# A fused convolution and feed-forward kernel: head slots shifted, chunks of 103 tokens

## The chip, the cores and the metric

One core of one Trainium2 chip. The metric is the device time of one execution in microseconds (us). The kernel before takes 484.77 us (median of 3 runs, 483.08 to 486.48). These three spread by 0.7%.

## The reference, cut to what matters

```python
# x: (8, 4160, 192), 8 heads of 24 channels, 7 taps per head, softmax over the taps
x_pad = concat(zeros(B, 6, D), x)                       # causal
conv[b, s, h, :] = sum_k w[h, k] * x_pad[b, s + k, h, :]
# then a feed-forward layer on the 33,280 tokens, 192 -> 768 -> 192
h = max(max(y @ w1, y @ w2), y @ w3)
out = h @ w_out
```

## The kernel before

Tokens are worked through in 65 blocks of 512. For each block the convolution runs on TensorE: a chunk of x (tokens in partitions) is the stationary operand, a banded matrix of the taps is the moving one, and the result comes out with channels in partitions. A chunk of n output tokens needs n + 6 input rows, and the rows of a chunk are the partitions of its load.

```python
CHK = P - PAD                       # 128 - 6 = 122 tokens, so 128 rows
...
for o_lo in range(0, N, CHK):       # 4 x 122 + 24
    o_hi = min(o_lo + CHK, N)
    row_lo = max(0, S + o_lo - PAD)
    rlen = min(P, SEQ - row_lo)
...
# load_x(t): all chunks of a block with one transfer where the rows allow it
src = bass.AP(tensor=x.tensor, offset=row[i] * D,
              ap=[[D, rlen], [step * D, k - i + 1], [1, D]])
nc.sync.dma_start(out=xf[0:rlen, i:k + 1, :], in_=src)
```

Each head's 24 channels fill a slot of 32 partitions, four slots to a PSUM bank. After evacuation to half precision (`ys`), transfers move the slots to a dense layout (`yd`, 64 channels in three columns), and one more transfer copies the lower 64 partitions to the upper 64, so that the matmuls of the two halves overlap: in the trace of before the 1170 `lp` and the 1170 `lq`, of 64 rows each, are busy 316.5 and 315.1 us, and together 347.5 us.

```python
def repack(t):                      # 10 pieces of 24, 16 or 8 rows
    for n, (half, s0, c, r0, rows) in enumerate(pieces):
        (nc.sync, nc.gpsimd)[n % 2].dma_start(out=yd[r0:r0 + rows, c, :],
                                              in_=slots[t][s0:s0 + rows, half, :])
def double(t):
    nc.sync.dma_start(out=dense[t][HALF:P, :, :], in_=dense[t][0:HALF, :, :])
...
for t in range(1, NB):
    u = t + AHEAD                   # AHEAD = 3
    load_x(t + 7)                   # sync queue
    cast_x(t + 5)                   # GpSimd
    double(u - 1)                   # sync queue
    l1(t, 0)                        # first matmuls of block t
    ...                             # conv(u), every second t for two blocks; evacuation
    repack(u)                       # sync queue and GpSimd
    ...                             # the rest of block t and of the second layer of t - 1
    store(t - 1, 0, 4, (nc.gpsimd,))
```

The softmax here doesn't subtract the row's maximum and nothing guards it: scores larger than these inputs give would overflow.

## Time and profile before

| | before |
|---|---|
| time | 484.77 us |
| TensorE busy | 470.7 us of 482.2 |
| period of two blocks | 14.0 us |
| x load of a block | 480 KB, 640 rows of 768 B |
| moves of a block's repack | 10 (5 sync queue, 5 GpSimd) |

One view is added here: the sync queue's instructions in order of time (start, duration, engine, line, kind, what goes where, how many).

```profile
65.66 0.54 SPq L365 DMA_DIRECT2D yd<-yd  x1
66.30 3.59 SPq L359 DMA_DIRECT2D yd<-ys  x5
69.93 0.52 SPq L123 DMA_DIRECT2D xf<-in_x_dram  x1
```

A block is one copy to the upper half, five moves of the repack and one load. The durations are those of issuing, not of moving data: 640 rows are issued in 0.52 us, and the last raise of such a load's semaphore comes 4.3 us after its issue (median).

### The profile page before, as it was taken

The page shows a single profiled execution, that of the slowest core. Times are in us where ns is not written, and L with a number is a line of the kernel's source. Part 1 is how long each engine was busy: PE and PEld are TensorE (multiplying, and loading weights), DVE is VectorE, ACT ScalarE, POOL GpSimd, SP SyncE. Part 2 cuts the span into 40 slices and gives each one's busy share as a digit, 9 for nine tenths or more (in the row PEclk, how much of TensorE's full clock was granted, in tenths as well). Part 3 has the DMA queues.
Part 4 walks back from the last instruction along what each step waited for, and adds up shares of the span by engine and source line. Part 5 has one row for each costly group of instructions (what it writes and reads, how often), then busy time and mean ns, then how long its engine had stood idle before and what let it go on. Part 6 is the DMA issues. An engine that isn't in the chain of part 4 may idle for free.

```text
span 482.2 us, 22628 instructions
## 1 busy us (share of the span) xinstructions
PE 470.7 (98%) x9083; PEld 394.6 (82%) x9083; DVE 367.3 (76%) x609; ACT 327.7 (68%) x608; POOL 279.1 (58%) x465
## 2 busy tenths in 40 slices
PE   7899999989999999999999999999999999999995
PEld 3478888878888888888888888888888888888995
DVE  6667877767778778777877777777877787787774
ACT  5676667756667676667677676766667666766663
POOL 2676656755655665575566557376755655676301
PEclk9899999999999999999999999999999999999999
DMA  8857756756666676666666676577665665664323
GB/s 203 242 153 201 197 155 190 204 152 186 199 185 184 175 200 183 177 191 176 194 198 190 190 193 190 159 196 215 201 170 167 207 189 164 194 164 112 95 83 100
DMA packets 77260, 85.86 MB, mean 178 GB/s; under 512 B 13472, under 2 KB 65160, under 8 KB 77156
## 3 DMA queue, kind: packets, MB, share of 16 engines
q1 hardware_dynamic: 59554, 52.74, 40.5%
q0 software_dynamic: 17248, 31.39, 21.0%
q8 instruction: 71, 1.16, 1.0%
q10 hardware_dynamic: 354, 0.30, 0.2%
q14 instruction: 33, 0.27, 0.2%
HBM read 34.04 MB, written 25.56 MB: 124 GB/s over the span
## 4 chain that ended last, share of the span: by engine, by line
PE 93%; DMA 3%; ACT 1%; DVE 1%; SPq 1%; issue 0%; POOL 0%; POOLq 0%
PE lp L376 30%; PE po L419 29%; PE lq L376 25%; PE G L310 7%; DMA yd<-yd 2%; DMA yd<-ys 1%; PE D L330 1%; PE idle L189 1%; SPq L359 1%; ACT r L380 0%; PE band_sum L234 0%; ACT band L257 0%; POOL yd L359 0%; ACT w3h L251 0%; DVE h L381 0%
## 5 line engine op out<-in xcount | busy, mean ns | idle before, releaser
L381 DVE TENSOR_TENSOR h<-r,lq 128x512 f16<-128x512 f16 x390 | 267.0, 685 | 103.5 <-ACT r L380 103.4
L380 ACT ACTIVATE r<-lp 128x512 f16<-128x512 f32 x390 | 232.7, 597 | 135.9 <-PE lp L376 93.8
L376 PE MATMUL lq<-yd,wd 64*128 64x512 f16 x1170 | 315.1, 375 | 1.8 <-DMA yd<-yd 1.3
L376 PE MATMUL lp<-yd,wd 64*128 64x512 f16 x1170 | 316.5, 377 | 0.1
L419 PE MATMUL po<-wo,h 64*128 64x192 f16 x3120 | 231.5, 243 | 0.0
L419 PEld LDWEIGHTS <-h 64*128 64x128 f16 x3120 | 187.2, 94 | 25.7 <-issue 0.2
L376 PEld LDWEIGHTS <-wd 64*128 64x128 f16 x2340 | 163.0, 93 | 26.0 <-DMA yd<-yd 2.9
L359 POOL DMA_DIRECT2D yd<-ys x315 | 161.6, 520 | 6.0 <-DMA yd<-ys 2.9
L445 POOL DMA_DIRECT2D out_dram<-o x64 | 51.3, 802 | 175.5 <-DVE o L429 145.0
L419 PE MATMUL po<-m,yd 64*128 64x192 f16 x780 | 87.0, 243 | 0.0
L429 DVE TENSOR_TENSOR o<-a,po 128x384 f32<-128x384 f32 (+1 forms) x132 | 71.3, 541 | 0.6 <-ACT a L428 0.6
L139 POOL CAST x<-xf 128x960 f16<-128x960 f32 (+3 forms) x71 | 64.2, 911 | 4.1 <-DMA xf<-in_x_dram 2.7
L428 ACT COPY a<-po 128x384 f32<-128x384 f32 (+1 forms) x132 | 61.8, 469 | 1.2 <-PE po L419 1.2
L419 PEld LDWEIGHTS <-yd 64*128 64x128 f16 x780 | 55.0, 94 | 6.1
L310 PEld LDWEIGHTS <-x 128*32 128x32 f16 (+1 forms) x2544 | 33.2, 97 | 13.0 <-issue 12.8
L341 ACT CAST ys<-G 128x512 f16<-128x512 f32 x66 | 36.3, 588 | 4.6 <-PE G L310 1.2
L341 DVE CAST ys<-G 128x512 f16<-128x512 f32 x60 | 38.5, 683 | 0.6 <-DMA yd<-ys 0.2
L310 PE MATMUL G<-band,x 128*32 128x122 f16 (+1 forms) x2544 | 36.4, 210 | 0.0
L154 POOL CAST xz<-xf 128x240 f16<-128x240 f32 (+2 forms) x6 | 2.4, 448 | 11.7 <-DMA xf<-in_x_dram 11.7
L189 PE MATMUL idle<-idle 128*128 128x512 f16 x14 | 6.1, 580 | 1.2 <-DVE unit L201 1.2
L189 PEld LDWEIGHTS <-idle 128*128 128x128 f16 x14 | 1.6, 131 | 3.6 <-issue 2.1
L330 PEld LDWEIGHTS <-xz 128*32 128x32 f16 x240 | 3.5, 102 | 1.3 <-issue 1.3
(43 smaller groups left out, 39.5 us busy)
## 6 DMA issues: line engine op xcount, KB each, us to landing
out_dram<-o POOLq DMA_DIRECT2D x64, 384.0 KB
xf<-in_x_dram SPq DMA_DIRECT2D x48, 480.0 KB
yd<-yd SPq DMA_DIRECT2D x63, 192.0 KB
yd<-ys SPq DMA_DIRECT2D x189, 24.0 KB
yd<-ys POOLq DMA_DIRECT2D x189, 24.0 KB
xf<-in_x_dram SPq DMA_DIRECT2D x8, 384.0 KB
xf<-in_x_dram SPq DMA_DIRECT2D x8, 288.0 KB
xf<-in_x_dram SPq DMA_DIRECT2D x8, 192.0 KB
```

Of the source, the lines that this page charges most:

```text
L139: nc.gpsimd.tensor_copy(out=x16[0:rl, q0:q1, :], in_=xf[0:rl, q0:q1, :])
L189: nc.tensor.matmul(ps[:], lhsT=idle[:, 0:P], rhs=idle[:], start=True, stop=True)
L310: nc.tensor.matmul(G[h // 4][32 * g:32 * g + 32, lo:hi], lhsT=x16[0:rlen, q, cb:cb + 32], rhs=band[0:rlen, h, cc:cc + hi - lo], start=True ...
L341: copy(out=slots[t][:, i, :], in_=convs[t][i][:])
L359: (nc.sync, nc.gpsimd)[n % 2].dma_start(out=yd[r0:r0 + rows, c, :], in_=slots[t][s0:s0 + rows, half, :])
L376: nc.tensor.matmul(ps[i][:, 0:N], lhsT=wd[row, c, P * j:P * (j + 1)], rhs=y[row, c, 0:N], start=(c == 0), stop=(c == NC - 1))
L380: nc.scalar.activation(out=r[:, 0:N], in_=ps[0][:, 0:N], func=AF.Relu)
L381: nc.vector.tensor_max(out=hs[t][:, j, 0:N], in0=r[:, 0:N], in1=ps[1][:, 0:N])
L419: nc.tensor.matmul(ps[b0, i][:, s % 2, :], lhsT=a, rhs=b, start=first, stop=last)
L428: nc.scalar.copy(out=a[:, ss, :], in_=ps[s0, 0][:, ss, :])
L429: nc.vector.tensor_add(out=outs[t][:, s0:s + 1, :], in0=a[:, ss, :], in1=ps[s0, 1][:, ss, :])
L445: qs[i].dma_start(out=bass.AP(tensor=out.tensor, offset=r * D, ap=[[D, n], [step * D, s1 - s0], [1, D]]), in_=ob[p0:p0 + n, s0:s1, :])
```

## The change

The intent is to have fewer and larger moves. Even heads are put at the end of their slot and odd heads at its start, so two neighbours touch and move together as 48 rows; the 10 moves become 6. To allow it the x tiles get 8 spare columns at each end. With it the chunks become even: 103, 103, 103, 103 and 100 tokens instead of 4 x 122 + 24.

```diff
-CHK = P - PAD
+CHK = 103
...
-                rlen = min(P, SEQ - row_lo)
+                rlen = min(CHK + PAD, SEQ - row_lo)
...
-            for h in range(NHEAD):
-                g = h % 4
-                cb = GRP * h if h < NHEAD - 1 else GRP * h - 8
-                nc.tensor.matmul(
-                    G[h // 4][32 * g:32 * g + 32, lo:hi],
-                    lhsT=x16[0:rlen, q, cb:cb + 32],
...
+            for i in range(2):
+                for g in range(4):
+                    h = SLOTS[i][g]          # ((0, 1, 2, 3), (6, 7, 4, 5))
+                    cb = q * D + GRP * h + EDGE * (g % 2)
+                    nc.tensor.matmul(
+                        G[i][32 * g:32 * g + 32, lo:hi],
+                        lhsT=x16[0:rlen, cb:cb + 32],
...
+    pieces = ((0, 8, 0, 0, 48), (0, 72, 0, 48, 16), (0, 88, 1, 0, 32),
+              (1, 72, 1, 32, 32), (1, 104, 2, 0, 16), (1, 8, 2, 16, 48))
```

Cut: the four x tiles in half precision become constants with their edges set to zero, and the cast writes between the edges.

More of the change, by code (lines that the diff above doesn't have):

```diff
@@ L87 @@
     xfp = ctx.enter_context(tc.tile_pool(name="xfp", bufs=6))
-    x16p = ctx.enter_context(tc.tile_pool(name="x16p", bufs=4))
     ysp = ctx.enter_context(tc.tile_pool(name="ysp", bufs=4))
@@ L100 @@
     NDENSE, AHEAD = 2, 3
+    SLOTS = ((0, 1, 2, 3), (6, 7, 4, 5))
+    EDGE = 32 - GRP
     xin = {}
+    nlast = len(chunks_of[NB - 1])
+    x16s = [const.tile([P, NQ * D + 2 * EDGE], FP16, name=f"x16_{i}") for i in range(4)]
+    x16z = const.tile([P, nlast * D + 2 * EDGE], FP16, name="x16_z")
     def load_x(t):
@@ L135, in cast_x @@
         n = len(chunks_of[t])
-        x16 = (x16p.tile([P, NQ, D], FP16, tag="x16", name=f"x16_{t}") if n <= NQ else
-               const.tile([P, n, D], FP16, name=f"x16_{t}"))
+        x16 = x16s[t % 4] if n <= NQ else x16z
+        v = x16[:, EDGE:EDGE + n * D].rearrange("p (q d) -> p q d", d=D)
         for (rl, q0, q1) in parts:
-            nc.gpsimd.tensor_copy(out=x16[0:rl, q0:q1, :], in_=xf[0:rl, q0:q1, :])
+            nc.gpsimd.tensor_copy(out=v[0:rl, q0:q1, :], in_=xf[0:rl, q0:q1, :])
         xin[t][1] = x16
@@ L195 @@
     nc.gpsimd.memset(xz[1][:], 0.0)
+    for x16 in x16s + [x16z]:
+        w = x16.shape[1] - EDGE
+        nc.gpsimd.memset(x16[:, 0:EDGE], 0.0)
+        nc.gpsimd.memset(x16[:, w:w + EDGE], 0.0)
     unit = const.tile([P, 32 + 2 * PAD], FP16)
@@ L306, in conv @@
         for (q, b, row_lo, rlen, lo, hi, cc) in chunks_of[t]:
-            for h in range(NHEAD):
-                g = h % 4
-                cb = GRP * h if h < NHEAD - 1 else GRP * h - 8
-                nc.tensor.matmul(
-                    G[h // 4][32 * g:32 * g + 32, lo:hi],
-                    lhsT=x16[0:rlen, q, cb:cb + 32],
-                    rhs=band[0:rlen, h, cc:cc + hi - lo],
-                    start=True, stop=True, tile_position=(0, 32 * g))
+            for i in range(2):
[5 more added lines that the diff above has]
+                        lhsT=x16[0:rlen, cb:cb + 32],
+                        rhs=band[0:rlen, h, cc:cc + hi - lo],
+                        start=True, stop=True, tile_position=(0, 32 * g))
         slots[t] = ysp.tile([P, 2, NBLK], FP16, tag="ys", name=f"ys_{t}")
@@ L341, in evac @@
         copy(out=slots[t][:, i, :], in_=convs[t][i][:])
-    pieces = []
-    for h in range(NHEAD):
-        s0 = 32 * (h % 4) + (8 if h == NHEAD - 1 else 0)
-        ch = GRP * h
-        while ch < GRP * (h + 1):
-            n = min(GRP * (h + 1), HALF * (ch // HALF + 1)) - ch
-            pieces.append((h // 4, s0 + ch - GRP * h, ch // HALF, ch % HALF, n))
-            ch += n
+    pieces = ((0, 8, 0, 0, 48), (0, 72, 0, 48, 16), (0, 88, 1, 0, 32),
+              (1, 72, 1, 32, 32), (1, 104, 2, 0, 16), (1, 8, 2, 16, 48))
     def repack(t):
```

## The prediction

> **What bounds the kernel now.** I read the head of the page first, then the chain that ended last, then the groups kept apart by shape.
>
> ```profile
> PE 470.7 (98%) x9083; PEld 394.6 (82%) x9083; DVE 367.3 (76%) x609; ACT 327.7 (68%) x608; POOL 279.1 (58%) x465
> ...
> q1 hardware_dynamic: 59554, 52.74, 40.5%
> q0 software_dynamic: 17248, 31.39, 21.0%
> ...
> PE 93%; DMA 3%; ACT 1%; DVE 1%; SPq 1%; issue 0%; POOL 0%; POOLq 0%
> ```
>
> TensorE is the bound: busy in 98% of the span and 93% of the chain. The windows view of 60 to 74 us and 200 to 214 us shows PE busy 14.00 of 14.00 us at clock 1.00. Two blocks of 512 tokens take 14.0 us there, so a block takes **7.0 us**, and 65 blocks with start and end make 482 us. The transfers are hidden: 40.5% + 21.0% of the 16 engines' time. That is an average over 16 engines, and the argument below turns on its not staying one.
>
> What the change touches, by shape:
>
> ```profile
> L359 POOL DMA_DIRECT2D yd<-ys x315 | 161.6, 520 | 6.0 <-DMA yd<-ys 2.9 <-issue 1.8 <-ACT ys L341 0.7
> L310 PE MATMUL G<-band,x 128*32 128x122 f16 x1984 | 34.6, 219 | 0.0
> L310 PE MATMUL G<-band,x 128*32 128x24 f16 x432 | 11.6, 175 | 0.0
> L139 POOL CAST x<-xf 94x192 f16<-94x192 f32 x8 | 2.8, 352 | 1.4 <-DMA xf<-in_x_dram 1.4
> ```
>
> The repack is 10 moves per block, 5 issued from GpSimd at 520 ns and 5 from the sync queue at 740 ns (median of the line's view). Neither queue is full. The last row is the only load with an odd row count, and it is the clue.
>
> **How a load is spread over the engines.** [...]Counting its semaphore records between a transfer's issue and its landing, a 128-row load raises its semaphore 16 times; the 94-row load (94 = 2 x 47) 3 times, one of them 0.5 us after issue[...] and two at 4.3 to 5.9 us; the 70-row load 15 times (14 engines + 1); the 24-row moves of the sync queue 13 times (12 + 1); the 8-row ones 9 (8 + 1). Some 10% of the small moves show fewer raises than their kind's number; one 70-row load and the eight 94-row loads are the only odd ones[...].
>
> The DMA view of 254.9 to 255.3 us, in the tail of a 94-row load, shows how fast two engines are:
>
> ```profile
> DMA packets 28, 0.02 MB, mean 56 GB/s; under 512 B 2, under 2 KB 27, under 8 KB 28
> ...
> q1 hardware_dynamic: 28, 0.02, 19.5%
> ```
>
> 27 - 2 = 25 packets are of 768 B (192 floats: one row of one chunk). On two engines over 0.4 us that is 0.4 x 2 / 25 = 32 ns each. In another such tail the packet records are two trains, each with a packet every **33 ns**. One engine moves one 768 B row per 33 ns.
>
> **The trap in the change.** A chunk of 103 tokens with its 6 rows before it is 109 rows, and **109 is prime**. The instruction order of the changed kernel shows every x load of the first 64 blocks on the sync queue as 109x5x192 (or 109x2 and 109x3). [...]all 5 x 109 = 545 packets of a block go through engine 0. Before, 5 x 128 = 640 packets went over 16 engines, 40 each, about 1.4 us.
>
> **The change part by part, per block.**
> - x load: 545 x 33 ns = **18.0 us** on engine 0. That alone is more than twice PE's 7.0 us, so it can't be hidden. It saves 15% of the bytes, which is worthless here.
> - Other traffic of engine 0: from the packet records (median alone): repack 192 rows x 1 KB = 12 packets per engine x 46 ns = 0.55; the copy to the lower half 4 packets of 3 KB x 121 ns = 0.48; store 5 packets of 4.6 KB x 178 ns and a smaller one of 65 ns = 0.95; about ten increments of 9 ns = 0.1. Sum 2.1 us. The new repack pieces of 16, 32 and 48 rows all use 16 engines, so this part is well spread.
> - So engine 0 needs **20.1 us per block** against PE's 7.0.
> - Repack: 4 fewer issues: 2 x 740 ns on the sync queue, 2 x 520 ns on GpSimd. None lies on the path before (GpSimd is 58% busy) and none will after.
> - Conv: still 40 pairs of weight load and matmul per block, 512 columns in all; 4 x 122 + 24 becomes 4 x 103 + 100. The chain gives 1.06 us for a pair of blocks (80 matmuls), 13 ns each. Even chunks can move this by some 0.1 us a block, at most 6 us, and it is hidden under 20 us.
> - Casts: 960 elements per partition as before, 0.99 us; ten tiny memsets at the start.
>
> **Does engine 0 stay fed?** At the start of the kernel before, loads are issued faster than they drain:
>
> ```profile
> 5.18 0.60 SPq L123 DMA_DIRECT2D xf<-in_x_dram  x1
> 7.27 0.37 SPq L179 DMA_DIRECT2D wos<-in_moe_w_out_dram  x1
> 7.69 8.50 SPq L123 DMA_DIRECT2D xf<-in_x_dram  x4
> ```
>
> Four issues take 8.50 us instead of 4 x 0.52. [...]rows issued less packets started, at the end of each held issue, come to 123 to 126 per engine. So a load of 545 rows holds the sync queue until some 124 are left, 124 x 33 ns = 4.1 us of work. In that time it must issue the copy (0.53), three repack moves (3 x 0.74) and the next load, whose first packet comes 1.18 us after its issue starts (spacing seen on isolated loads): 0.53 + 2.2 + 1.18 = 3.9 us. It just fits, and the copy and repack packets add 0.75 us of cover. Gaps of up to 1 us a block are possible. The repack's evacuations are ready long before, since PE works only 7 of 20 us.
>
> **The sum.** First packet at 1.9 us; x packets of 64 blocks 64 x 18.0 = 1151; weights' share of engine 0 some 6 (some 110 rows of 768 B to 2 KB); other traffic of the 57 blocks finished meanwhile 57 x 2.1 = 120. The copy of block t+2 is issued behind the load of block t+7 in the same ring, so PE enters block 58 only when the load of block 63 is through: 1279 us. From there PE runs as before: block 58 starts at about 427 us of 482, so 55 us remain, plus 2 for the copy's landing. 1279 + 57 = 1336. I add 14 for gaps and for a PE that may be cold after each wait: **1350 us**, 2.8 times the time before.
>
> **Rivals.**
> - *The spread is not what I think* (the next dimension is used, or a ragged split over 16 engines). Then 409 KB per block are hidden as 480 were, and only fewer DMAs, even conv chunks and smoother starts count. DMA waits on PE's own records are 1.7 us in all, so 476 to 484 us: within 2%. For it: 94 and 70 rows show divisors, but no prime count is in this trace. Against: 94 gave 2 and not 16, though 16 engines were there, and 24 gave 12. I give it 6%.
> - *Engine 0 starves between loads*: the sync queue waits for a repack to land before the copy, and then first packets come late: 1.2 to 2 us per block, 64 x 1.5 = 96, about 1430 us.
> - *Rows are slower than 33 ns in a long train.* With all 16 engines on loads at 13.3 to 16.2 us, 1242 packets take 2.9 x 16 / 1242 = 37 ns each, which would make 64 x 545 x 37 = 1290 and 1475 in all. [...]alone two engines kept 33, so I hold it unlikely.
> - *DVE, ACT or GpSimd as new bound*: no; they do the same work as before in a longer time, and would be some 25% busy.
>
> **Range and chances.** Both slower rivals set the top of the range, 1460; the bottom, 1300, is the sum with 32 ns and less other traffic. Faster 0.01, same 0.05, slower 0.94.
>
> **What would show it.** PE busy near 35% (471 of 1350 us; more where a colder clock stretches it), its idle put down to DMA (yd<-yd above all), and a clock below 1 in slices. The sync queue's line of x loads with a median near 14 us in place of 0.5. Of all engines' time the DMA share down to some 16% (18 + 16 x 2.1 = 52 of 16 x 20.1 us a block), and mean bandwidth near 60 GB/s (85.9 MB less 15% of the loads' 31 MB, over 1350 us). A period of 20 us per block instead of 7. Two raises of the semaphore per x load, the first at once, the second some 20 us later. Wrong if x loads still land in 4 us, or if the period is far from 20 us: at 18 the other traffic overlaps, at 22 or more the ring ran dry.

The sum: 1.9 + 1151 + 6 + 120 = 1279, plus 57 is 1336, plus 14 is 1350 us. What the trace of before shows is the count of raises: 16 for 128 rows, 3 for 94, 15 for 70, and in the sync queue's moves 13 for 24 rows and 9 for 8. 94, 70, 24 and 8 rows raise once more than their largest divisor up to 16. For the 94-row loads one raise comes 0.5 us after the issue, and the first packet of an isolated load only after 1.18 us, so I count the others as engines, and 16 raises as 16. That 109 rows would leave one engine was my estimate from these counts; no prime row count was in that trace, and the changed kernel's trace shows it below. "Engine 0" is a name for that one engine, as no trace names a packet's engine, and "ring" one for the queue. That 16, 32 and 48 rows use 16 engines is read from 16 raises each in the sync queue of the changed kernel. That a colder TensorE stretches its work shows there too: the same 9083 matmuls keep it busy 609.4 us at a mean granted clock of 0.709, against 470.7 us at 0.995 before.

## More of the kernel before

Where the data's arrival matters, it shows in somebody's wait. Of who waited for whom, two of the lines, GpSimd's casts for x and TensorE's first matmuls for the copy, are:

```profile
POOL x L139 <- DMA xf<-in_x_dram: 2.7, 4, 1.4
...
PE lq L376 <- DMA yd<-yd: 1.3, 2, 1.1
```

These are totals over the whole execution in us, number of times, and the longest. Both are small, so the transfers are hidden.

## The result, and the profile after

The changed kernel takes **1338.04 us** (median of 4 runs, 1337.43 to 1338.99), against 485.26 us for 4 runs of before. The ratio is 2.7589 (95% interval 2.7484 to 2.7693). A ratio here is the mean time of one kernel's fast runs over that of the other's of the same rounds, so it is not quite the ratio of the medians.

From the head of the page of the changed kernel: busy time by engine, the two main queues (packets, MB, share of 16 engines) and the chain by engine.

```profile
PE 609.4 (46%) x9083; PEld 432.7 (32%) x9083; DVE 374.8 (28%) x609; ACT 333.6 (25%) x608; POOL 212.6 (16%) x341
...
q1 hardware_dynamic: 51894, 48.27, 12.7%
q0 software_dynamic: 13216, 31.38, 6.3%
...
DMA 63%; SPq 27%; PE 4%; issue 3%; POOL 1%; POOLq 0%; ACT 0%; DVE 0%
```

TensorE does the same 9083 matmuls and is busy 46% instead of 98%. The transfers' share of all engines has fallen from 61.5% to 19.0%, and yet the chain is 63% transfers. Low mean use of 16 engines and a bound by transfers do not exclude each other: one engine can be full. The DMA view of 605 to 611 us, inside one x load, shows it:

```profile
DMA packets 181, 0.14 MB, mean 23 GB/s; under 512 B 4, under 2 KB 179, under 8 KB 181
...
q1 hardware_dynamic: 174, 0.13, 6.5%
```

For 6 us on end the core moves 23 GB/s, and the share is 6.5%, which is one sixteenth (6.25%). 174 packets in 6 us are one per 34 ns. Of who waited for whom, the lines that answer to those of before:

```profile
POOL x L146 <- DMA xf<-in_x_dram: 551.8, 62, 17.0
...
PE lq L383 <- DMA yd<-yd: 629.3, 57, 28.4
```

GpSimd's cast waits for x 62 times, and TensorE waits 57 times, once a block, for the copy. The copy is not slow in itself (with the loads in another queue, in e10 below, it lands 5.1 us after its issue; here 19.3, medians). It stands behind a load of x in the same queue, which the sync queue's order of time shows:

```profile
618.58 13.50 SPq L372 DMA_DIRECT2D yd<-yd  x1
632.13 1.86 SPq L366 DMA_DIRECT2D yd<-ys  x3
634.04 6.84 SPq L130 DMA_DIRECT2D xf<-in_x_dram  x2
641.11 10.78 SPq L372 DMA_DIRECT2D yd<-yd  x1
651.98 1.82 SPq L366 DMA_DIRECT2D yd<-ys  x3
653.85 0.43 SPq L130 DMA_DIRECT2D xf<-in_x_dram  x1
658.39 14.38 SPq L372 DMA_DIRECT2D yd<-yd  x1
```

From copy to copy two blocks take 658.39 - 618.58 = 39.8 us, so 19.9 a block. The load's own issue is 0.43 us; the instruction after it, the copy, is held for 13.5 to 14.4 us. (Where a load is issued in two parts, the x2 line, the second part is held too, and the copy for 10.8 us.) The trace's semaphore records say how many engines a load used: all 72 loads of 109 rows raise their semaphore exactly twice, at medians of 0.6 and 23.1 us after the issue; without the early one that is one engine, as the 6.5% says. The 70-row load of the last block raises it 15 times.

### The profile page after: what moved, and what is told of

The parts are those of the page before. It is cut to its first block, busy times and chain, and to the rows that moved or that the text cites. A ratio compares the mean times of both kernels' runs of the same rounds, so it can differ in the third digit from the quotient of the medians.

```text
span 1335.5 us, 21944 instructions
## 1 busy us (share of the span) xinstructions
PE 609.4 (46%) x9083; PEld 432.7 (32%) x9083; DVE 374.8 (28%) x609; ACT 333.6 (25%) x608; POOL 212.6 (16%) x341
## 4 chain that ended last, share of the span: by engine, by line
DMA 63%; SPq 27%; PE 4%; issue 3%; POOL 1%; POOLq 0%; ACT 0%; DVE 0%
DMA xf<-in_x_dram 53%; SPq L372 17%; DMA yd<-ys 9%; SPq L366 4%; SPq L130 3%; SPq L186 2%; PE po L426 2%; DMA yd<-yd 1%; PE lp L383 1%; POOL yd L366 1%; PE lq L383 1%; SPq L171 1%; PE G L322 0%; POOL x L146 0%; POOLq L366 0%
## 5 line engine op out<-in xcount | busy, mean ns | idle before, releaser
L383 PE MATMUL lq<-yd,wd 64*128 64x512 f16 x1170 | 389.5, 448 | 629.3 <-DMA yd<-yd 629.3
L383 PEld LDWEIGHTS <-wd 64*128 64x128 f16 x2340 | 170.5, 106 | 716.5 <-DMA yd<-yd 645.9
L383 PE MATMUL lp<-yd,wd 64*128 64x512 f16 x1170 | 390.5, 440 | 14.4 <-DMA yd<-ys 14.2
L426 PE MATMUL po<-wo,h 64*128 64x192 f16 x3120 | 289.8, 265 | 0.0
L426 PEld LDWEIGHTS <-h 64*128 64x128 f16 x3120 | 218.8, 105 | 48.6 <-issue 18.0
L146 POOL CAST x<-xf 109x960 f16<-109x960 f32 x62 | 61.2, 987 | 551.8 <-DMA xf<-in_x_dram 551.8
L426 PE MATMUL po<-m,yd 64*128 64x192 f16 x780 | 120.9, 277 | 0.0
L366 POOL DMA_DIRECT2D yd<-ys x189 | 95.5, 509 | 106.9 <-ACT ys L353 71.9
L322 PE MATMUL G<-band,x 109*32 109x103 f16 (+1 forms) x2480 | 59.2, 287 | 43.9 <-POOL x L146 43.9
L322 PEld LDWEIGHTS <-x 109*32 109x32 f16 x2480 | 52.1, 142 | 70.0 <-POOL x L146 68.8
L353 DVE CAST ys<-G 128x512 f16<-128x512 f32 x60 | 38.7, 686 | 26.8 <-PE G L322 24.9
L342 PEld LDWEIGHTS <-xz 109*32 109x32 f16 x240 | 5.4, 143 | 28.4 <-ACT xz L161 14.4
```

The lines of the kernel that those rows point to most:

```text
L146: nc.gpsimd.tensor_copy(out=v[0:rl, q0:q1, :], in_=xf[0:rl, q0:q1, :])
L322: nc.tensor.matmul(G[i][32 * g:32 * g + 32, lo:hi], lhsT=x16[0:rlen, cb:cb + 32], rhs=band[0:rlen, h, cc:cc + hi - lo], start=True, stop=T ...
L353: copy(out=slots[t][:, i, :], in_=convs[t][i][:])
L383: nc.tensor.matmul(ps[i][:, 0:N], lhsT=wd[row, c, P * j:P * (j + 1)], rhs=y[row, c, 0:N], start=(c == 0), stop=(c == NC - 1))
L426: nc.tensor.matmul(ps[b0, i][:, s % 2, :], lhsT=a, rhs=b, start=first, stop=last)
```

## The experiments

Twelve kernels ran, and all twelve gave correct outputs. Before was run beside them in each group (medians 483.98 to 485.97 us).

### 112 rows loaded, the rest of the change kept (e1)

```diff
-                rlen = min(CHK + PAD, SEQ - row_lo)
+                rlen = min(112, SEQ - row_lo)
```

> The changed kernel with one number changed: 112 rows are loaded and cast per chunk instead of 109 (3 more than needed; the band's zeros take them out). Theory (the prime row count alone puts the loads on one engine): 112 divides by 16, each engine gets 35 packets of a load, the loads are hidden again and TensorE is the bound: 476 to 484 us, each load raises its semaphore 16 times. Rival (something else in the change costs the time: the new slots, the shared x tiles, odd chunks of 103): it stays near 1338 us or well above 500.

Measured: 482.33 us (6 runs), ratio to before 0.9954 (0.9926 to 0.9983). Each full load raises its semaphore 16 times. Three more rows per chunk, 15 rows more to move in a block, take 856 us off the time. The sync queue is as it was before:

```profile
69.92 0.50 SPq L372 DMA_DIRECT2D yd<-yd  x1
70.46 1.86 SPq L366 DMA_DIRECT2D yd<-ys  x3
72.37 0.67 SPq L130 DMA_DIRECT2D xf<-in_x_dram  x1
```

The new slots, the shared x tiles with their edges, the odd chunks of 103 and the matmuls are all still there, so none of them is the cause.

### Chunks of 106 tokens (e2)

```diff
-CHK = 103
+CHK = 106
```

> The changed kernel with chunks of 106 tokens, so that 106 + 6 = 112 rows are all needed (4 x 106 + 88 tokens). Theory: as e1, 476 to 484 us, and within 1% of e1. Rival: as in e1, well above 500.

Measured: 482.19 us (6 runs), ratio 0.9964 (0.9929 to 0.9999). It is the same as e1. It saves no rows: it too loads 5 x 112 rows a block where 542 are needed, with the spare ones all in the last chunk (88 tokens need 94 rows).

### The two intended parts alone (e3, e4)

e3 is the changed kernel with `CHK = P - PAD` and `rlen = min(P, ...)` as before. e4 is the kernel before with `CHK = 103` and 112 rows.

> The new head slots and the repack in 6 moves, with the chunks of 122 tokens and 128 rows of before. Theory: the repack was hidden, so within 1% of before (480 to 487 us). Rival (the 10 moves cost something on the path): 2% or more faster, below 475.

Measured: 482.81 us (6 runs), ratio 0.9968 (0.9938 to 0.9999).

> The kernel before, with its slots and 10 moves, but chunks of 103 tokens loaded as 112 rows. Theory: within 1.5% of before (477 to 487 us): the conv is 40 pairs a block either way. Rival (even chunks save the issue of short matmuls): the conv of a pair of blocks falls from 1.06 to about 0.9 us and the time by some 5 us.

Measured: 484.20 us (6 runs), ratio 0.9996 (0.9960 to 1.0033). The conv of two blocks in the chain went from 1.06 to 1.03 us, not to 0.9; that rival falls. The repack was hidden in before. Its new form takes GpSimd's busy time from 279 to 213 us. The ratio says 0.3%, at most 0.6% by the interval, whose upper end nearly touches 1.

### Other row counts (e5, e6, e7)

Each is the changed kernel with one number for the rows of a load: 118 = 2 x 59, 111 = 3 x 37, 115 = 5 x 23. These vary the number of engines while all but the row count stays.

> The changed kernel with 118 = 2 x 59 rows loaded per chunk. Theory: 2 engines, 295 packets x 33 ns = 9.7 us a load, so 2 + 6 + 64 x 9.7 + 57 x 2.1 + 57 = 808 us; three raises of the semaphore per load. Rival (the time follows the bytes or rows of a load, not a divisor): slower than 1338 us, by 8% more rows, about 1430.

> The changed kernel with 111 = 3 x 37 rows. Theory: 3 engines, 185 packets x 33 ns = 6.1 us a load, with 2.1 us of other traffic 8.2 us a block, still over TensorE's 7.0: 2 + 6 + 64 x 6.1 + 57 x 2.1 + 57 = 576 us. Rival (time follows rows): about 1360 us.

> The changed kernel with 115 = 5 x 23 rows. Theory: 5 engines, 115 packets x 33 ns = 3.8 us, with 2.1 us of other traffic 5.9 us a block, under TensorE's 7.0: the loads are hidden, 478 to 490 us though 11 engines move no x at all. Rival (a load must be spread over all 16 engines to be hidden): well over 500 us.

| rows | engines (raises less 1; 16 raises are 16) | packets per engine | load at 33 ns | expected | measured |
|---|---|---|---|---|---|
| 109 | 1 | 545 | 18.0 us | 1350 | 1338.04 |
| 118 | 2 | 295 | 9.7 us | 808 | 820.86 |
| 111 | 3 | 185 | 6.1 us | 576 | 593.57 |
| 115 | 5 | 115 | 3.8 us | 478 to 490 | 497.76 |
| 112 | 16 | 35 | 1.2 us | 476 to 484 | 482.33 |

(e5 to e7 are medians of 2 runs.) The number of raises is 3, 4 and 6, so 2, 3 and 5 engines. With 2 and 3 engines the time is 1.6% and 3.1% over the sum, which was not followed up. More rows make the kernel faster when they have a larger divisor: 118 rows take 517 us less than 109. The rival that time follows rows or bytes falls.

e7 missed its range by 8 us and is not "well over 500" as its rival said; against before its verdict is unclear (ratio 1.0254, 1.0131 to 1.0378). Its chain shows where the time went. The conv of a pair of blocks recurs every 13.95 us, as in e1, so the loads of the steady part are hidden on 5 engines:

```profile
202.72 1.03 PE G L322 x72
216.67 1.03 PE G L322 x72
230.62 1.03 PE G L322 x70
```

The last such pair starts at 453.79 us against 439.17 in e1, and the second one at 63.25 against 48.38. The 15 us are there from the beginning: they are lost at the start, where loads and weights are queued together (e7's whole chain has 2.9% of the span in issuing x loads, 2.4% in their landing and 1.7% in that of weights). The sum had no term for that once loads are hidden.

### 127 rows in the kernel before (e8), and the moves again (e11, e12)

e8 is the kernel before with `CHK = 121`, so 127 rows. e11 is the changed kernel with `CHK = 121`. e12 is the kernel before with `CHK = 103` and 109 rows.

> The kernel before with one token less per chunk: 121 tokens, so 127 rows, a prime, and its own slots and 10 moves. Theory: one engine, 5 x 127 = 635 packets x 33 ns = 21.0 us a load: 2 + 6 + 64 x 21.0 + 57 x 2.1 + 57 = 1527 us, slower than the changed kernel. Rival (the slots or the shared x tiles of the change are needed for the loss): about 485 us.

Measured: 1595.50 us (2 runs). One token less per chunk in the kernel before makes it take 3.3 times as long, so the change's own edits are not needed for the loss. The size was missed by 68 us. My sum forgot that in 8 blocks the last chunk has 98 rows (15 raises, so 14 engines by the same count), which lowers it to 1494; the true miss is 101 us. e11 and e12 were made to find it.

> The changed kernel (new slots, 6 moves) with chunks of 121 tokens and so 127 rows. 56 blocks have 635 packets on engine 0 and 8 blocks 508 + 7 (their last chunk has 98 rows, 14 engines): 39,680 x 33 ns = 1309 us, and with 2 + 6 + 57 x 2.1 + 57 in all 1494 us. Theory A (the run with 127 rows and 10 moves was over its sum because 5 moves between two loads on the sync queue let engine 0 run dry): about 1494, within 1.5%. Theory B (rows of a 127-row load are slower themselves): about 1580 to 1600, as with 10 moves.

Measured: 1498.02 us (2 runs).

> The kernel before with chunks of 103 tokens and 109 rows, and its own slots and 10 moves. Main theory: about the time of the changed kernel, 1338 us, as the repack has no part in the loss. Theory A adds to it that 10 moves let engine 0 run dry: 1380 to 1410 us. Theory B (rows of 127 are slow, not the moves): 1338, within 1%. Rival to both (slots or shared x tiles make the loss): about 485.

Measured: 1399.94 us (2 runs).

| | 6 moves | 10 moves |
|---|---|---|
| 109 rows | 1338.04 | 1399.94 |
| 127 rows | 1498.02 | 1595.50 |

With 6 moves the sum holds for both row counts (1494 for 127). With 10 moves 62 and 97 us come on top, so theory B (rows of 127 are slow) falls, and so does e12's main theory (the repack has no part in the loss). What remains is the form of the repack: the 10 moves with their slots and tile places. e12 lies in theory A's range, 1380 to 1410, but that is partly luck, since the one engine running dry is only a part of it. The sync queue of e12:

```profile
623.93 3.58 SPq L359 DMA_DIRECT2D yd<-ys  x5
627.56 0.42 SPq L123 DMA_DIRECT2D xf<-in_x_dram  x1
630.44 13.47 SPq L365 DMA_DIRECT2D yd<-yd  x1
```

Five moves take 3.58 us between two loads where three take 1.86. I went through the packet records of the part that the loads bind (from 130 us on, up to 1270 in the changed kernel and 1330 in e12), taking the time between x packets. In e12 no packet at all was moving for 12.5 us, against 0.8 in the changed kernel; other packets filled 130 us against 109; and over the whole span 11,138 rows came 34 to 60 ns after the last one, against 369, which adds 31 us against 3 over a 33 ns pace. These three differences, each good to a few us, make 61 of the 62 us. The first, 12 us, is the engine running dry. (The same count for 127 rows, e8 against e11, gives 39, 23 and 31 of the 97 us, so there it is a larger part.) For the second there is only an estimate: the sync queue's moves of 24 and 8 rows raise 13 and 9 times in before, so 12 and 8 engines, against 16 raises for each of its moves in the changed kernel; if the engine of the rows is always among the 12 and the 8, it carries more. That is not shown, as the trace doesn't name a packet's engine. Why a third of the rows come a little slower in both kernels with 10 moves, and not in those with 6, stays open; they differ in the places of the tiles too.

### The x loads from another engine (e9, e10)

```diff
-            nc.sync.dma_start(out=xf[0:rlen, i:k + 1, :], in_=src)
+            nc.gpsimd.dma_start(out=xf[0:rlen, i:k + 1, :], in_=src)    # e9; nc.scalar in e10
```

> The changed kernel, 109 rows, with the x loads issued from GpSimd instead of the sync queue. Theory: [...]35 packets an engine and some 480 to 490 us. Rival (109 rows go to one engine whoever issues them): about 1340 us.

Measured: 1525.15 us (2 runs). The theory (a load from GpSimd is spread over 16 engines) falls: 109 rows are one train from GpSimd too. Its semaphore does rise 16 times, but that is no sign of 16 engines here. The DMA view of 614 to 619 us, inside a load:

```profile
DMA packets 28, 0.13 MB, mean 27 GB/s; under 512 B 0, under 2 KB 0, under 8 KB 27
...
q0 software_dynamic: 27, 0.12, 6.4%
```

27 packets of 4608 B (six rows) in 5 us are one per 185 ns, and 6.4% is one engine. That is 24.9 GB/s, where single rows from the sync queue made 768 B per 33 ns = 23.3 GB/s. The load of 545 rows is 90 such packets and one of five rows; beside them the block has 1350 packets of 24 B, 15 for each of the 90. A block takes 25 us, from one load issue of GpSimd to the next (621.29 and 646.31 us). It is slower than the changed kernel since the train stops: once a block no large packet starts for some 6 us (621.5 to 627.8 us here; 62 pauses over 2 us make 380 us). Why it stops is not shown; GpSimd sits idle for 869.2 us before its x issues, with no release that the profile shows.

> The changed kernel, 109 rows, with the x loads issued from the ScalarE queue, so that copies and repack moves no longer stand behind them in one queue. Theory (engine 0's 20.1 us a block set the time, not the sync queue that is held): nearly the same, 1300 to 1345 us; up to 35 us less, as the copy of block t+2 need not wait for the load of block t+7 and TensorE ends closer behind the last load. Rival (the sync queue being held for 13.5 us a block is the bound itself): below 1000 us, or ScalarE is held and everything is slower than 1400.

Measured: 1404.97 us (2 runs). That is over the theory's 1300 to 1345 and inside the rival's second branch (ScalarE held, slower than 1400), so the time alone doesn't decide; the trace does. With the loads in ScalarE's queue the copies are no longer held: their issue has a median of 0.50 us and they land 5.1 us after issue instead of 19.3. It gains nothing: from 130 to 1330 us the rows, and other packets between them, fill all but 61 of 1200 us. So the train of rows still sets the pace, which refutes that the held sync queue was the bound. Instead ScalarE is held by its own next load:

```profile
630.42 8.88 ACTq L130 DMA_DIRECT2D xf<-in_x_dram  x1
639.40 0.60 ACT L387 ACTIVATE r<-lp 128x512 f16<-128x512 f32 x1 [8.56 <-issue]
```

Its activations and evacuations come late, TensorE waits 667.9 us for ScalarE in all, and the train of rows has those 61 us of gaps in which nothing moved, against 0.8 in the changed kernel. That is about the 67 us by which e10 is slower.

## Why the prediction was right

The time (1350 said, 1338 measured) and the mechanism came out as written. Point by point:

- **Spread of a load.** One engine for 109 rows: two raises for each of 72 loads, 6.5% of 16 engines in a load, and 482 us at 112 rows. The raises for 109, 118, 111 and 115 rows (2, 3, 4 and 6) are again one more than the largest divisor up to 16, and 112 rows raise 16 times; the times are in the table above. For 127 rows the sum with one engine gave 1494 us, and e11 took 1498.02.
- **Pace of 33 ns.** The median distance of x packets in the changed kernel is 33 ns, as in the tails of 94-row loads before. The rival with 37 ns in a long train is refuted.
- **The sum.** The one-engine loads of x end at 1278.7 us by the packet records (1279 said), and 56.7 us follow to the end of the span (57 said). The first packet came at 1.77 us (1.9). Other packets filled 109 us between rows from 130 us on (120 said for the whole). That the end fits within 1 us is partly luck: the share that is not rows was 11 us before 130 us and 115 after, where the sum had 6 for the weights and 120. The 14 us added for gaps were not needed.
- **The one engine stays fed.** In the changed kernel nothing moved for 0.8 us in 1140. The working had the sync queue held until some 124 rows are left: at the ends of three held issues of before 123 to 126 rows per engine were issued and not started (145 after the one before them, which was not held), and at the ends of 56 held copies of the changed kernel 112 to 123 rows. The margin was as thin as the working said: with 10 moves in place of 6 (e12) dry gaps appear.
- **Signs in the profile.** Period 19.9 us (20.1). The second raise of a load's semaphore came at a median of 23.1 us after its issue (some 20). Mean 61 GB/s (60). TensorE busy 46% (35% or more if colder): the mean clock was 0.709 (0.71 from 130 to 1270 us, 1.00 from 1290 to 1330 us, when no load is left), and the conv of blocks 61 and 62, right after the last such wait, kept TensorE busy 1.91 us against 1.13 for a pair before. DMA share 19.0% on the two main queues (16 said); the records of other packets are longer than the 121 ns and the like that the working took from packets alone, for instance 222 ns on average for the copy's 3 KB.
- **One step failed in its place.** The prediction had the x load's own line at a median near 14 us. It is 0.43 us; the hold falls on the next transfer of the same queue, the copy (13.62 us median). The size was right: (545 - 124) x 33 ns = 13.9 us.
- **A reading that was incomplete.** The 94-row and 70-row loads are not the only ones of before with fewer than 16 raises: a recount finds 12, 13 and 14 at three 128-row loads, and fewer than their kind's number at 6% of the small moves (10% said). Some records seem to be missing there, but all eight 94-row loads show 3.
- **The share of the intent.** "Not on the path" was right: the two parts without the prime are within 0.5% of before (e1 to e4).

## What to carry to other kernels

Before changing a tile's rows, factor the row count: in the sync queue's loads here the engines counted by raises were its largest divisor up to 16 (109 rows: 1, 118: 2, 111: 3, 115: 5, 112: 16; in time 1338.04, 820.86, 593.57, 497.76 and 482.33 us), 127 rows took 1498.02 us with the same moves, and from ScalarE's queue 109 rows were one train as well (1404.97 us). Rounding 109 up to 112, a multiple of 16, cost nothing that shows (482.33 us, 483.98 before). Check it in the trace by counting a semaphore's raises (not for loads from GpSimd, where 16 raises stood for one train), or by a DMA share stuck at one sixteenth. A transfer that looks hidden by an average over 16 engines must be held against the block's period on its fullest engine (18.0 us of rows against 7.0 us here), and a load need not use all engines, only enough (5 sufficed in the steady part of e7: 13.95 us for two blocks, as in e1).
